# Decimating a complex recurrence by four instead of two: one short scan, three phases by diagonal products on the TensorE, and state reloads on one queue

## The chip, the cores and the metric

The kernel runs on one core of one Trainium2 chip. The metric is the device time of one execution in microseconds (us). Executions of a kernel agree within one or two per cent here (449.45 to 457.46 us for the kernel before), and runs more than 1.5% above the fastest of their kernel are called slow and are left out of ratios. Every ratio below is the mean time of one kernel's fast runs over the mean of the fast runs of the kernel before in the same rounds on the same chip, so it is not quite the ratio of the medians that are quoted. Brackets hold its 95% interval.

Engines: PE is the TensorE's matmuls, PEld its weight loads (they overlap the matmuls: 422.9 and 242.3 us busy in a span of 451.4 us), DVE the VectorE, ACT the ScalarE, POOL the GpSimd, SP the SyncE, which here does nothing but issue DMAs. SPq is its queue. In this code an eviction copies a finished product out of PSUM into SBUF, the on-chip memory; a scatter is a DMA that spreads a result over other partitions; the hole is the one long stretch in which PE stands idle.

## The reference, cut to what matters

S = 2048 steps, D = 1024 channels, P = 1024 complex states, batch 1. Branch a is a complex diagonal recurrence, branch b is a short convolution, a product with v and a long convolution by FFT over 4096 points; a gate mixes both.

```python
def _A_ref(x, ...):
    Lam_bar = jnp.exp(dt * Lam)                       # complex, one per state
    B_bar = ((Lam_bar - 1.0) / Lam)[:, None] * Bmat
    Bu = jnp.einsum("bld,pd->blp", x + 0j, B_bar)
    for t in range(L):
        h = Lam_bar[None, :] * h + Bu[:, t, :]
        hs.append(h)
    return 2.0 * jnp.einsum("blp,dp->bld", hseq, Cmat).real + x * Dskip
def _B_ref(q, k, v, ...):
    kv = k_shift * v                                  # k_shift: 4-tap causal convolution of k
    y = irfft(rfft(kv, 4096) * rfft(ssm_k, 4096))[:S] + kv * ssm_D
    return q * y
g = sigmoid((x * gate_w).sum(-1, keepdims=True))
return g * a + (1 - g) * b                            # q is x
```

## The kernel before

Nearly all big work is matmuls. A small list scheduler in Python (`_Plan`) is given every operation with an engine, a duration, a priority and the buffers it touches; it fixes the order of instructions on every engine, and where each buffer lies in SBUF, before the kernel is built. Some fifty constants (priorities, numbers of buffers) steer it. An elementwise operation with `alt=("POOL", ...)` may be given to POOL instead of DVE, until the planned time `PUNTIL`.

The states are handled in eight blocks of 128. For each block the 2048 steps are split by parity. Odd steps' inputs are folded into even steps by a product with 128x128 diagonal matrices (a complex factor takes four), a scan on DVE runs over even steps only, after a rotation that makes its factor real, and the odd steps follow by another product.

```python
xT = [pl.tile("xT", [2, SE], cap=8) for d in range(ND)]       # SE = 1024, CW = 512, NC = 2
for par in (1, 0):
    for d in range(ND):
        dma("SP", 1.3, ... xT[d].ap[:, par, :] <- xf[par:S:2, d * 128:(d + 1) * 128],
            ..., transpose=True, issue=1.9)                    # 16 transposes of 1024 steps
...
def prep(pi, bn, pr):
    dg = pl.tile("dg", [6, 128], cap=3)                        # six diagonal matrices
    ...
        op("DVE", 0.97, mk(V), ..., alt=("POOL", 1.5, mk(G), PUNTIL))
...
def gemm_u(BT, dg, Hc, par, c, pr, step=8):                    # 16 products B u for 512 steps ...
    ...
    if par == 0:                                               # ... and the odd inputs folded in
        for ri in range(2):
            for k in range(2):
                PE_.matmul(ps.ap[:, ri, 1:CW], lhsT=dg.ap[:, LMAT[ri][k], :],
                           rhs=Hc[c].ap[:, 1, k, 0:CW - 1], ...)
                if c > 0: ...                                  # one column across the seam
...
def rot(Hc, pi, c, tab, wl, pr):                               # DVE, for each chunk c of 512
    ...                                                        # rotate
    V.tensor_tensor_scan(out=W.ap[:, ri, :], data0=col(r2, pi).to_broadcast([128, CW]), ...)
    ...                                                        # rotate back
def odd(dg, Hc, pi, c, pr):
    for ri in range(2):
        PE_.matmul(ps.ap[:, ri, :], lhsT=ident, rhs=Hc[c].ap[:, 1, ri, :], start=True, stop=False)
        for k in range(2):
            PE_.matmul(ps.ap[:, ri, :], lhsT=dg.ap[:, LMAT[ri][k], :], rhs=Hc[c].ap[:, 0, k, :], ...)
    ...
    if pi < NP - NKEEP:                                        # NKEEP = 4 blocks of H stay on chip
        dma(QB, ...)                                           # the others go to HBM
...
for i, pi in enumerate(korder):
    load_CT(pi, 0, CTP(i, 0))                                  # C transposed, first half
    ...
        t = pl.tile("Hr", [2, 2, CW], cap=16, hold=True)
        dma(QB, 1.6, ..., alt=QA)                              # reload, 512 KB; QB, QA = "POOL", "SP"
```

At the end 32 output products of 16 matmuls each (line L1097, L1085 in the changed kernel) contract all eight blocks of H with C. Each needs H of every block and all of C's half. The last units of branch b run beside them; a unit makes several trips: products, an eviction, elementwise work, a DMA that scatters the result over partitions, and a final product (L782, L784 in the changed kernel) that waits for this scatter.

Of the kernel before, what the change touches and what calls it, by code (L numbers as in the profile page):

```python
# [15 lines left out]
MAGIC = 12582912.0  # L16
# [296 lines left out]
def kernel(  # L313
# [31 lines left out]
    SE = S // 2  # L345
    CW = 512
    NC = SE // CW
# [11 lines left out]
    h_scr = dram.tile([NP, NC, 128, 4 * CW], BF16, name="h_scr")  # L359
    g_scr = dram.tile([2, SE], F32, name="g_scr")  # L360
# [42 lines left out]
    dco = parm.tile([128, NP, 6], F32, name="dco")  # L403
# [23 lines left out]
    r2 = small("r2")  # L427
    mul(r2, rv, rv)
# [13 lines left out]
    TS(out=phn, in0=thn, scalar1=-2.0, scalar2=None, op0=ALU.mult)  # L442
# [23 lines left out]
    phU = small("phU")  # L466
    TS(out=phU, in0=phn, scalar1=float(CW), scalar2=None, op0=ALU.mult)
    rqU = small("rqU")
    TS(out=rqU, in0=phU, scalar1=MAGIC, scalar2=-MAGIC, op0=ALU.add, op1=ALU.add)
    TT(out=phU, in0=phU, in1=rqU, op=ALU.subtract)  # L470
    sU = small("sU")
    nc.scalar.activation(out=sU, in_=phU, func=ACT.Sin, scale=TWO_PI)
    faU = small("faU")
    nc.scalar.activation(out=faU, in_=phU, func=ACT.Abs)
    cU = small("cU")
    nc.scalar.activation(out=cU, in_=faU, func=ACT.Sin, bias=pihalf_col, scale=-TWO_PI)
    msU = small("msU")
    TS(out=msU, in0=sU, scalar1=-1.0, scalar2=None, op0=ALU.mult)
# [47 lines left out]
    XE = -856.08  # L526
    F1P = -578.83
    NSPL = 1
    NWARM = 12
    GP0 = -22.93  # L530
    GP1 = -182.81
    GP2 = -79.99
    BNCAP = 31
    PUNTIL = 41.5
    ZBCAP = 2
    NKEEP = 4
    HCAP = 5
    TABCAP = 15
    ZCAP = 20
    KVCAP = 23  # L540
    QQCAP = 6
    RACAP = 15
    RBCAP = 13
    KTCAP = 1
    ABCAP = 1
    PPCAP = 1
# [3 lines left out]
    S0 = 29.93  # L550
    S1 = 1.34
    C0 = 39.78
    C1 = 2.56
    CB1 = -1.01
    CT0 = 218.24
    CT1 = 3.6
    CT2 = 310.87
    SPARE = 1
    NBIG = 3
    HR0 = 41.49  # L560
    HRc = -154.4
    KP0 = -267.98
    KP1 = -0.01
    KPu = -27.09
    KA0 = -122.57
    VA0 = -112.74
    FN0 = -2.02
    TB0 = -166.71
    TB1 = 13.16
    XS0 = -149.35  # L570
    PN0 = -1.23
    RT0 = 13.76
    OD0 = -6.8
    UE0 = 6.92
    D10 = -557.08
    SC1 = 2.49
# [11 lines left out]
    xT = [pl.tile("xT", [2, SE], cap=8) for d in range(ND)]  # L588
    for par in (1, 0):
        for d in range(ND):  # L590
            dma("SP", 1.3, lambda d=d, par=par: [xT[d].ap[:, par, :]],
                lambda d=d, par=par: [xf[par:S:2, d * 128:(d + 1) * 128]], [], [(xT[d], par)], (-1000 if par else XE) + d, transpose=True, issue=1.9)
# [222 lines left out]
    def s5(prio):  # L815
        LMAT = ((3, 5), (4, 3))
# [7 lines left out]
        def prep(pi, bn, pr):  # L824
            dg = pl.tile("dg", [6, 128], cap=3)
            def mk(eng):
                return lambda: eng.tensor_tensor(out=dg.ap, in0=ident.unsqueeze(1).to_broadcast([128, 6, 128]),
                                                 in1=dco[:, pi, :].unsqueeze(2).to_broadcast([128, 6, 128]), op=ALU.mult)
            if pi == 0:
                for k in range(2):  # L830
                    def part(k=k):
                        V.tensor_tensor(out=dg.ap[:, 3 * k:3 * k + 3, :], in0=ident.unsqueeze(1).to_broadcast([128, 3, 128]),
                                        in1=dco[:, pi, 3 * k:3 * k + 3].unsqueeze(2).to_broadcast([128, 3, 128]), op=ALU.mult)
                    op("DVE", 0.5, part, r=[e_dco], w=[(dg, k)], prio=pr - 5)
            else:
                op("DVE", 0.97, mk(V), r=[e_dco], w=[(dg, 0), (dg, 1)], prio=pr - 5, alt=("POOL", 1.5, mk(G), PUNTIL))
# [39 lines left out]
        def gemm_u(BT, dg, Hc, par, c, pr, step=8):  # L876
            ps = pl.psum([2, CW])
            c0 = c * CW

            def part(ds):  # L880
                def f():
                    for ri in range(2):
                        for d in ds:
                            PE_.matmul(ps.ap[:, ri, :], lhsT=BT.ap[:, d, ri, :], rhs=xT[d].ap[:, par, c0:c0 + CW],  # L884
                                       start=(d == 0), stop=(par == 1 and d == ND - 1))
                op("PE", 2 * len(ds) * MM(512), f, r=[BT] + [(xT[d], par) for d in ds], w=[ps], prio=pr)
            for d0 in range(0, ND, step):
                part(range(d0, d0 + step))
            if par == 0:
                def g():  # L890
                    for ri in range(2):
                        for k in range(2):
                            lm = dg.ap[:, LMAT[ri][k], :]
                            PE_.matmul(ps.ap[:, ri, 1:CW], lhsT=lm, rhs=Hc[c].ap[:, 1, k, 0:CW - 1], start=False,  # L894
                                       stop=(c == 0 and k == 1))
                            if c > 0:
                                PE_.matmul(ps.ap[:, ri, 0:1], lhsT=lm, rhs=Hc[c - 1].ap[:, 1, k, CW - 1:CW],
                                           start=False, stop=(k == 1))
                op("PE", 4 * MM(511) + (0.2 if c else 0), g, r=[(dg, 1), (Hc[c], 1)] + ([(Hc[c - 1], 1)] if c else []), w=[ps],
                   prio=pr)  # L900
            evac(lambda: Hc[c].ap[:, par], lambda: ps.ap, r=[ps], w=[(Hc[c], par)], prio=pr)

        def rot(Hc, pi, c, tab, wl, pr):
            t1 = pl.tile("ra", [2, CW], cap=RACAP)
            t2 = pl.tile("rb", [2, CW], cap=RBCAP)
            H = Hc[c]
# [15 lines left out]
            def g():  # L922
                init = (0.0, 0.0)
                if c > 0:
                    STT = V.scalar_tensor_tensor
                    wb, wi, tq = wl.ap[:, 0:2], wl.ap[:, 2:4], wl.ap[:, 4:6]
                    TS(out=tq, in0=wb, scalar1=col(cU, pi), scalar2=None, op0=ALU.mult)
                    STT(out=wi[:, 0:1], in0=wb[:, 1:2], scalar=col(msU, pi), in1=tq[:, 0:1], op0=ALU.mult, op1=ALU.add)
                    STT(out=wi[:, 1:2], in0=wb[:, 0:1], scalar=col(sU, pi), in1=tq[:, 1:2], op0=ALU.mult, op1=ALU.add)
                    init = (wi[:, 0:1], wi[:, 1:2])  # L930
                for ri in range(2):
                    V.tensor_tensor_scan(out=W.ap[:, ri, :], data0=col(r2, pi).to_broadcast([128, CW]),
                                         data1=t1.ap[:, ri, :], initial=init[ri], op0=ALU.mult, op1=ALU.add)
                if c < NC - 1:
                    V.tensor_copy(wl.ap[:, 0:2], W.ap[:, :, CW - 1])
# [28 lines left out]
        def gates(pr):  # L964
            for par in (1, 0):
                gate1(par, pr[par])
# [17 lines left out]
        def gate1(par, pr):  # L984
# [13 lines left out]
            if par == 1:  # L998
                wps = pl.psum([128])
# [158 lines left out]
```

## Time and profile before

| | kernel before |
|---|---|
| time, median of 3 | 453.71 us (451.0 to 455.12) |
| span of the profiled run | 451.4 us |
| PE, DVE, ACT, POOL busy | 94%, 77%, 65%, 7% |
| mean granted clock | 0.986 |

These are lines of the page of the kernel before: busy time and share of each engine, and PE, POOL and the granted clock in 40 slices of 11.3 us (tenths).

```profile
PE 422.9 (94%) x2859; PEld 242.3 (54%) x2906; DVE 345.6 (77%) x624; ACT 291.2 (65%) x330; POOL 32.6 (7%) x49
...
PE   8799999999999999998999999199999999999995
...
POOL 9800101000101000000000002000000000000000
PEclk9999999999999999999999999779999999999999
```

PE is the engine that bounds, with one hole (the 1) near 280 us. This is a line of PE's timeline in the kernel before: start, us, engine, line, operation, out<-in, shapes, how many.

```profile
321.71 3.62 PE L1097 MATMUL ps<-slab,slab 128*128 128x512 bf16 x16
```

The page gives 379 ns as the mean of one such matmul, but matmuls overlap. Sixteen of them took 3.62 us, of which the last one's own 0.38 us belong to its end, so they start every (3.62 - 0.38) / 15 = 0.216 us: this is the price of 512 streamed columns. With this price one can count what PE really streams in each stage, and what is missing. These are stretches of the kernel before: window, its length, then busy us (count) of PE, PEld, DVE, ACT and POOL, granted clock, DMA share, GB/s.

```profile
20.00:60.00 40.00, 37.23 (x203) 16.64 (x207) 30.00 (x49) 31.75 (x32) 3.60 (x6) 1.00 0.95 182
60.00:120.00 60.00, 57.88 (x411) 34.90 (x418) 56.45 (x98) 50.03 (x53) 5.41 (x10) 1.00 0.82 187
120.00:280.00 160.00, 155.80 (x1134) 94.76 (x1150) 145.04 (x266) 136.74 (x149) 6.38 (x12) 1.00 0.73 159
280.00:300.00 20.00, 9.93 (x68) 5.84 (x67) 7.37 (x13) 7.86 (x10) 0.00 (x0) 0.74 0.96 269
300.00:360.00 60.00, 58.98 (x445) 36.75 (x450) 53.07 (x88) 39.09 (x45) 0.00 (x0) 1.00 0.75 166
```

At 280 to 300 us PE is busy 9.93 of 20 us, and the clock falls to 0.74. The waits of PE in the kernel before name the cause (us in total, times, longest):

```profile
PE ps L782 <- DMA slab<-slab: 11.1, 2, 10.0
PE ps L990 <- DMA slab<-in_A_x_dram: 3.1, 2, 2.2
```

Final products of a unit waited 10.0 us for their scatter. These are lines of the timeline of SP in the kernel before (start, us, what was issued), and after them one of POOL's:

```profile
276.89 5.88 SPq L509 DMA_DIRECT2D slab<-slab  x4
...
286.03 6.71 SPq L509 DMA_DIRECT2D slab<-h_scr  x2
```

```profile
276.63 2.62 POOL L509 DMA_DIRECT2D slab<-h_scr  x5 [0.33 <-PE ps L884]
```

The four parts of the scatter were issued at 276.89, just when POOL issued five reloads of 512 KB in a row.

### The profile page before, as it was taken

The page shows a single profiled execution, that of the slowest core. Times are in us where ns is not written, and L with a number is a line of the kernel's source. Part 1 is how long each engine was busy: PE and PEld are TensorE (multiplying, and loading weights), DVE is VectorE, ACT ScalarE, POOL GpSimd, SP SyncE. Part 2 cuts the span into 40 slices and gives each one's busy share as a digit, 9 for nine tenths or more (in the row PEclk, how much of TensorE's full clock was granted, in tenths as well). Part 3 has the DMA queues.
Part 4 walks back from the last instruction along what each step waited for, and adds up shares of the span by engine and source line. Part 5 has one row for each costly group of instructions (what it writes and reads, how often), then busy time and mean ns, then how long its engine had stood idle before and what let it go on. Part 6 is the DMA issues. An engine that isn't in the chain of part 4 may idle for free.

```text
span 451.4 us, 7616 instructions
## 1 busy us (share of the span) xinstructions
PE 422.9 (94%) x2859; PEld 242.3 (54%) x2906; DVE 345.6 (77%) x624; ACT 291.2 (65%) x330; POOL 32.6 (7%) x49
## 2 busy tenths in 40 slices
PE   8799999999999999998999999199999999999995
PEld 6533546665656546655665566155576544444442
DVE  5974999989999599988998889079998654464412
ACT  3675979887888978997888878268576122321200
POOL 9800101000101000000000002000000000000000
PEclk9999999999999999999999999779999999999999
DMA  8999574899867967494457389988866676353111
GB/s 155 99 249 223 96 198 129 187 239 166 214 157 162 261 134 188 102 229 101 111 158 130 84 153 257 291 212 160 168 149 163 174 206 168 118 163 94 55 39 46
DMA packets 169401, 72.12 MB, mean 160 GB/s; under 512 B 136514, under 2 KB 165202, under 8 KB 169364
## 3 DMA queue, kind: packets, MB, share of 16 engines
q1 hardware_dynamic: 165796, 59.80, 63.3%
q0 software_dynamic: 3504, 11.82, 8.1%
q8 instruction: 23, 0.38, 0.4%
q14 instruction: 14, 0.11, 0.1%
q10 hardware_dynamic: 64, 0.01, 0.0%
HBM read 29.65 MB, written 16.79 MB: 103 GB/s over the span
## 4 chain that ended last, share of the span: by engine, by line
PE 72%; DMA 10%; ACT 7%; SPq 6%; DVE 3%; issue 2%; DVEq 0%; ACTq 0%
PE ps L1097 24%; PE ps L884 20%; DMA slab<-slab 5%; ACT slab L514 5%; SPq L507 5%; PE ps L736 4%; PE ps L737 3%; PE ps L956 3%; PE ps L723 3%; PE ps L763 2%; PE ps L738 2%; DMA kv_scr<-slab 2%; PE ps L894 2%; DMA slab<-in_A_x_dram 2%; PE ps L782 2%
## 5 line engine op out<-in xcount | busy, mean ns | idle before, releaser
L514 ACT CAST slab<-ps 128x1024 bf16<-128x1024 f32 x217 | 205.5, 1032 | 82.4 <-PE ps L765 20.9
L884 PE MATMUL ps<-slab,slab 128*128 128x512 bf16 x486 | 114.1, 379 | 2.8 <-ACT slab L514 1.7
L1097 PE MATMUL ps<-slab,slab 128*128 128x512 bf16 x487 | 109.0, 379 | 0.5
L1097 PEld LDWEIGHTS <-slab 128*128 128x128 bf16 x512 | 49.9, 98 | 59.0 <-issue 0.2
L884 PEld LDWEIGHTS <-slab 128*128 128x128 bf16 x512 | 48.8, 98 | 59.4 <-issue 7.3
L1103 DVE SCALAR_TENSOR_TENSOR slab<-ps,gcols,slab 128x512 bf16<-128x512 f32 x32 | 23.2, 747 | 51.2 <-PE ps L1097 51.1
L1080 ACT ACTIVATE slab<-slab,omgc 128x512 bf16<-128x512 bf16 x32 | 21.3, 735 | 43.7 <-DMA slab<-pB_scr 43.7
L736 PE MATMUL ps<-slab,fC 128*128 128x512 bf16 x115 | 43.5, 379 | 0.8 <-DVE slab L1103 0.5
L514 DVE CAST slab<-ps 128x1024 bf16<-128x1024 f32 x23 | 27.9, 1221 | 11.0 <-PE ps L846 2.9
L737 PE MATMUL ps<-slab,fS 128*128 128x256 bf16 x128 | 34.9, 272 | 0.7
L738 PE MATMUL ps<-slab,fN 128*128 128x256 bf16 x128 | 34.9, 272 | 0.0
L723 PE MATMUL ps<-tab,slab 128*128 128x128 bf16 x512 | 34.0, 220 | 0.7 <-ACT slab L514 0.6
L723 PEld LDWEIGHTS <-slab 128*128 128x128 bf16 x512 | 31.0, 99 | 4.5 <-issue 1.3
L708 ACT ACTIVATE slab<-slab,skc 128x1024 bf16<-128x1024 bf16 (+3 forms) x28 | 32.2, 1164 | 0.2 <-DVE slab L710 0.2
L763 PE MATMUL ps<-slab,gC 128*128 128x256 bf16 x128 | 29.9, 273 | 1.9 <-ACT slab L514 1.4
L710 DVE TENSOR_TENSOR slab<-slab,slab 128x1024 bf16<-128x1024 bf16 (+3 forms) x45 | 30.7, 683 | 0.3 <-ACT slab L708 0.2
L765 PE MATMUL ps<-slab,gS 128*128 128x128 bf16 x128 | 28.0, 219 | 0.0
L764 PE MATMUL ps<-slab,gN 128*128 128x128 bf16 x128 | 28.0, 219 | 0.0
L753 DVE TENSOR_TENSOR slab<-slab 128x512 bf16<-128x512 bf16 x64 | 25.1, 417 | 0.3 <-DMA slab<-slab 0.2
L782 PE MATMUL ps<-slab,tabFc 128*128 128x512 bf16 x32 | 13.1, 409 | 11.1 <-DMA slab<-slab 11.1
L750 DVE TENSOR_TENSOR slab<-slab 128x1024 bf16<-128x1024 bf16 x32 | 21.9, 684 | 1.3 <-PE ps L956 1.3
L1085 DVE SCALAR_TENSOR_TENSOR slab<-slab,gcols,slab 128x512 bf16<-128x512 bf16 x32 | 22.4, 744 | 0.0
(178 smaller groups left out, 536.9 us busy)
## 6 DMA issues: line engine op xcount, KB each, us to landing
slab<-in_A_x_dram SPq DMA_DIRECT2D x32, 256.0 KB
slab<-slab SPq DMA_DIRECT2D x128, 64.0 KB
slab<-in_B_ssm_k_dram SPq DMA_DIRECT2D x8, 512.0 KB
kv_scr<-slab SPq DMA_DIRECT2D x8, 512.0 KB
h_scr<-slab POOLq DMA_DIRECT2D x8, 512.0 KB, 4.1
slab<-kv_scr SPq DMA_DIRECT2D x8, 512.0 KB
pB_scr<-slab SPq DMA_DIRECT2D x16, 256.0 KB
slab<-pB_scr SPq DMA_DIRECT2D x16, 256.0 KB
```

The costliest lines, as they stand in the source:

```text
L514: op("ACT", 1.04, lambda: A.copy(o_(), i_()), r=r, w=w, prio=prio, alt=("DVE", 1.2, lambda: V.tensor_copy(o_(), i_())))
L708: alt=("ACT", 1.17, lambda: A.activation(out=tmp.ap[:, 0:n], in_=kT.ap[:, src], func=ACT.Copy, scale=skc[:, u, j:j + 1])))
L710: op("DVE", 0.7, lambda: TT(out=acc.ap[:, lo:hi], in0=acc.ap[:, lo:hi], in1=tmp.ap[:, 0:n], op=ALU.add), r=[acc, tmp], w=[acc], prio=pr)
L723: PE_.matmul(ps.ap[:, i, :], lhsT=a.ap[:, 8 * q + i, :], rhs=t1v[:, hh * 128:(hh + 1) * 128], start=True, stop=True)
L736: PE_.matmul(ps.ap[:, i], lhsT=fC[:, k2, :], rhs=zz, start=True, stop=False)
L737: PE_.matmul(ps.ap[:, i, :, 0, :], lhsT=fS[:, k2, :], rhs=zz[:, :, 1, :], start=False, stop=False)
L738: PE_.matmul(ps.ap[:, i, :, 1, :], lhsT=fN[:, k2, :], rhs=zz[:, :, 0, :], start=False, stop=True)
L763: PE_.matmul(ps.ap[:, i], lhsT=gC[:, k2, :], rhs=pp.ap[:, i], start=True, stop=False)
L764: PE_.matmul(ps.ap[:, i, 0, :], lhsT=gN[:, k2, :], rhs=pp.ap[:, i, 1, :], start=False, stop=False)
L765: PE_.matmul(ps.ap[:, i, 1, :], lhsT=gS[:, k2, :], rhs=pp.ap[:, i, 0, :], start=False, stop=True)
L884: PE_.matmul(ps.ap[:, ri, :], lhsT=BT.ap[:, d, ri, :], rhs=xT[d].ap[:, par, c0:c0 + CW], start=(d == 0), stop=(par == 1 and d == ND - 1))
L1097: PE_.matmul(ps.ap[:, ti, :], lhsT=Hr[pi, a // 4].ap[:, par, ri, (a % 4) * 128:(a % 4 + 1) * 128], rhs=CT[pi, dh].ap[:, ri, :], start=(i = ...
```

## The change

The intent is to halve DVE's part of the recurrence. With four phases instead of two parities, one scan of 512 steps per block does what two scans of 512 did. PE pays: 12 diagonal matmuls instead of 8 fold three phases into phase 0, and a chain of three products of six matmuls each, with an eviction after each, gives the phases 1 to 3 instead of two products. H of six blocks instead of four stays on chip, so that four reloads are left instead of eight, and all four are issued by SP. x comes in as 32 transposes of 512 steps instead of 16 of 1024. `PUNTIL` rises, so POOL may take elementwise work longer. All constants were tuned again.

```diff
-    xT = [pl.tile("xT", [2, SE], cap=8) for d in range(ND)]
-    for par in (1, 0):
+    xT = [pl.tile("xT", [NPH, CW], cap=8) for d in range(ND)]          # NPH = 4
+    for ph in (1, 2, 3, 0):
         for d in range(ND):
-            dma("SP", 1.3, lambda d=d, par=par: [xT[d].ap[:, par, :]], ... xf[par:S:2, ...], issue=1.9)
+            dma("SP", 0.65, lambda d=d, ph=ph: [xT[d].ap[:, ph, :]], ... xf[ph:S:NPH, ...], issue=1.0)
...
-            dg = pl.tile("dg", [6, 128], cap=3)
+            dg = pl.tile("dg", [12, 128], cap=DGCAP)
+            def part(k, n, eng, dur, **kw):
+                ...
+                op("DVE", dur, f(V), ..., alt=("POOL", 1.9 * dur, f(G), PUNTIL))
+            part(0, 3, V, 0.5)
+            part(3, 9, V, 1.4)
...
-                        for k in range(2):                              # fold one phase: 4 matmuls
-                            PE_.matmul(ps.ap[:, ri, 1:CW], lhsT=lm, rhs=Hc[c].ap[:, 1, k, 0:CW - 1], ...)
+                        for j in range(1, NPH):                         # fold three phases: 12 matmuls
+                            for k in range(2):
+                                PE_.matmul(ps.ap[:, ri, 1:CW], lhsT=dg.ap[:, LM(j, ri, k), :],
+                                           rhs=H[(NPH - j) // 2].ap[:, (NPH - j) % 2, k, 0:CW - 1], ...)
...
-            for c in range(NC):
-                rot(Hc, pi, c, tab, wl, prio(b + RT0 + 4 * c))
-            for c in range(NC):
-                odd(dg, Hc, pi, c, prio(b + OD0 + 2 * c))
+            rot(Hc, pi, tab, prio(b + RT0))
+            for ph in (1, 2, 3):
+                chain(dg, Hc, ph, prio(b + OD0 + 2 * (ph - 1)))
...
-                    dma(QB, 1.6, ... h_scr[pi, c], ..., alt=QA)         # reload
+                    dma("SP", 1.8, ... h_scr[pi, c], ...)
...
-                        for _ in range(20):                             # warm-up matmuls
+                        for _ in range(12):
...
-    PUNTIL = 41.5
-    NKEEP = 4
-    CT0 = 218.24
+    PUNTIL = 126.82
+    NKEEP = 6
+    CT0 = 313.99                                                        # priority of C's transposes
...                                                                      # and about 45 more constants
```

## The prediction

> **What bounds it now.** PE. The busy table gives it 94%, but matmul ends are modelled, so I counted streamed columns: at 0.213 us for 512 columns (page's groups: 109 us for 512 output products) the program's order holds 406 us of columns, 9.8 of them warm-up, in a span of 451.4. The windows view shows the rest: 0-44 us (x and B arrive; last x at 43.8), PE busy 97% from 44 to 280, one hole at 280-300 (PE busy 9.9 of 20 us, granted clock 0.74), then PE full to 447. The waits view has one large PE wait after the start: 10.0 us of the final inverse matmuls for slab<-slab, the scatter of the inverse. By the timeline eight 512 KB reloads of H start around it, six in a burst on the POOL queue. DVE (77%) and ACT (65%) cost PE only waits under 1 us.
>
> **What the change does.**
> - PE: per 128 states 12 diagonal matmuls for phase 0 instead of 8, and 18 in the chain instead of 12: +80 x 0.213 = +17 us, all on the bounding engine. 32 one-column matmuls go, ~0.1 us each: -3. Eleven more switches to the one-row gate product, ~0.2 each: +2.
> - DVE: half of the rotations and scans go: per 512 steps 4 x 0.684 + 4 x 0.42 + 2.45 = 6.9 us, x 8 = -55 us, and -5 of seam work; but 29 more evictions stand on DVE (x 1.22 = +35). [...] DVE does not bound: worth 1-3 us.
> - DMA: H of six of eight state blocks stays on chip; four reloads instead of eight, in order on SP. The 10 us wait and the low clock after it (13 us of columns missing in 280-300) should mostly go: -9 to -13. But scatters now stand behind reloads and C transposes; between a unit's last inverse product and its final product only 8-11 us of columns lie (18.6 at the old hole): new waits of 1-5 us.
> - Start: 32 half-size x transposes. C transposes of that size take 1.2 us to issue, the large ones 1.28, so the last x lands at 44-47 us though the first phase is complete at about 15 instead of 27. Both orders place equal PE work before the last piece: -2 to +2.
>
> **Sum.** 451 + 17 - 3 + 2 - 12 - 2 + 1 = about 454; perfect packing would give 444. I put the time at **452 us**, 8 in 10 between **444 and 462**. Chances: faster by over 2% 0.10, within 2% 0.78, slower by over 2% 0.12.
>
> **What would show it.** PE columns up by 14 us, PE share 95% or more; DVE busy down by only 20-40 us; no PE wait of 10 us around the first output products, and full clock there, but waits of 1-5 us of final products for slab<-slab; last gate product at 44-47 us; the output stage starts later with fewer other matmuls inside.
>
> **What would make it wrong.** Faster: PE streams from 17 us and loses nothing later. Slower: the serial chain (scan, three products, an eviction between each) leaves PE nothing else ready; reloads waiting on SP for buffers block the scatters and open a new hole of 10 us; or half-size transposes cost more than half.

The prediction's small prices against the trace of the kernel before: a scan took 1.21 to 1.27 us (L932). The issue of a transpose of C took 1.20 to 1.21 us and that of a large one of x 1.30 us (medians). The two steps of a switch, from a product of 512 columns to the one-row gate product and back, took 0.309 and 0.310 us from start to start instead of 0.216, 0.19 us more in sum. The 0.1 us of a one-column matmul was the estimate: its weight load took 0.096 us (L897), but the next matmul starts 0.026 us after it.

## The result, and the profile after

The changed kernel is correct and slower.

| | before | after |
|---|---|---|
| time, median of 6 | 452.95 us | 466.82 us |
| ratio of fast runs | | 1.0336 [1.0274, 1.0398] |
| span of the profiled run | 451.4 us | 465.5 us |
| mean granted clock | 0.986 | 0.983 |

The same lines of the page, after:

```profile
PE 437.9 (94%) x2839; PEld 246.6 (53%) x2890; DVE 340.3 (73%) x552; ACT 269.6 (58%) x300; POOL 55.7 (12%) x54
...
PE   7869999889999999999999999996998999999995
...
POOL 9940103080251000000000000000000000000000
PEclk9897999998999999999999999999999999999999
```

PE's share is the same, and the hole near 280 us is gone. New dents stand near the start and near 315 us, and POOL is busy up to 140 us (the 8 and the 5). The stretches of the changed kernel (columns as before):

```profile
20.00:60.00 40.00, 35.63 (x174) 14.40 (x177) 32.85 (x46) 28.58 (x33) 10.31 (x10) 0.91 0.78 166
60.00:120.00 60.00, 56.01 (x394) 34.35 (x400) 56.17 (x79) 42.18 (x45) 15.33 (x13) 0.97 0.66 156
120.00:280.00 160.00, 158.95 (x1098) 94.42 (x1118) 140.61 (x225) 126.74 (x137) 11.60 (x9) 1.00 0.67 146
280.00:300.00 20.00, 19.84 (x153) 12.37 (x154) 8.87 (x15) 12.60 (x13) 0.00 (x0) 1.00 0.96 189
300.00:360.00 60.00, 52.13 (x409) 33.13 (x416) 42.67 (x65) 35.45 (x38) 0.00 (x0) 1.00 0.77 164
```

And the waits of PE in the changed kernel:

```profile
PE ps L980 <- ACT slab L514: 4.1, 1, 4.1
PE ps L725 <- DMA slab<-kv_scr: 3.6, 1, 3.6
PE ps L765 <- DVE slab L755: 3.3, 2, 2.4
PE ps L784 <- DMA slab<-slab: 2.8, 2, 1.8
PE ps L980 <- DMA slab<-in_A_x_dram: 2.6, 3, 1.1
```

Instead of one wait of 10 us there are five or six of 1 to 4 us. To add them up I counted, for each stage, the columns that PE streamed (records of weight loads by line, times the columns of that line, at 0.2133 us for 512, without the fixed part of a matmul) and took them from the length of the stage. Both parts of the price are read from the kernel before: its matmuls of 512 columns start 215.8 ns apart (mean of neighbours of L1097 from 120 to 440 us) and those of 128 columns 55.8 ns apart (L723; the group of 16 at 268.97 us took 1.06 us, (1.06 - 0.22) / 15 = 0.056). So 384 columns took 160.0 ns, which is 0.2133 us for 512, and about 2.5 ns are left that do not go with the columns. Warm-up matmuls do not count as useful. The rest is time that PE lacks, whether it waited, ran at a low clock (0.50 from 34 to 40 us, below) or paid the fixed part of each matmul. The 2.5 us that the changed kernel lacks from 120 to 280 us, with 1118 weight loads, are about this fixed part (an estimate: 1118 x 2.5 ns = 2.8 us): there the trace shows no wait of PE.

| lost in the stage, us | 0-20 | 20-60 | 60-120 | 120-280 | 280-300 | 300-360 | 360-end | sum | useful columns |
|---|---|---|---|---|---|---|---|---|---|
| before | 16.4 | 5.2 | 4.0 | 8.3 | 13.0 | 2.2 | 6.1 | 55.0 | 396.4 |
| after | 16.2 | 10.8 | 6.5 | 2.5 | 0.5 | 9.1 | 6.5 | 52.0 | 413.5 |
| difference | -0.2 | +5.6 | +2.5 | -5.8 | -12.5 | +6.9 | +0.4 | -3.0 | +17.1 |

The 14.1 us are 17.1 us of added columns less only 3.0 us of lost time won back. The hole gave its 12.5 us, but 5.6 us more are lost at 20-60 and 6.9 us more at 300-360.

Three readings show what stands there. First, x. The timeline of SP shows the issue of all transposes of x as one group, in the kernel before and then in the changed kernel:

```profile
0.73 36.41 SPq L507 DMA_TRANSPOSE slab<-in_A_x_dram  x16
```

```profile
0.73 43.73 SPq L507 DMA_TRANSPOSE slab<-in_A_x_dram  x32
```

The same 4 MB take 43.73 instead of 36.41 us: on average 1.37 us for a transpose of half the size, against 2.28 (43.73 / 32 and 36.41 / 16; the medians of a single issue are 1.26 and 1.30 us, the longest 2.2 and 6.8). The last gate product, which needs the last piece, ran at 49.3 instead of 43.8 us.

Second, DVE and POOL. The table computation of the FFT has the same tiny instruction in both kernels (16 elements per partition). Here it is in the kernel before, then two lines of DVE in the changed kernel, then what POOL did meanwhile in the changed kernel:

```profile
13.72 0.23 DVE L618 TENSOR_SCALAR slab<-iota_row,slab 128x16 f32<-128x16 f32 x1
```

```profile
21.12 3.96 DVE L620 TENSOR_SCALAR slab<-iota_row,slab 128x16 f32<-128x16 f32 x1
...
101.52 3.76 DVE L708 TENSOR_SCALAR slab<-slab,skc 128x1024 bf16<-128x1024 bf16 x1
```

```profile
14.85 6.15 POOL L832 TENSOR_TENSOR slab<-ident,dco 128x1152 bf16<-128x1152 bf16 x3 [0.82 <-DVE dco L477]
...
22.13 2.91 POOL L832 TENSOR_TENSOR slab<-ident,dco 128x384 bf16<-128x384 bf16 x2
...
102.07 2.91 POOL L832 TENSOR_TENSOR slab<-ident,dco 128x384 bf16<-128x384 bf16 x2
```

A DVE instruction of 0.23 us lasted 3.96 us until POOL's group at 22.13 had ended at 25.04, and the one of 3.76 us (0.48 us in after_no_pool below) ended at 105.28, after POOL's group at 102.07 had ended at 104.98. So these two ended only when POOL's products had ended; below this is called the stall. Not every instruction stalls: three products of DVE at 94.78, 96.53 and 97.14 us, beside POOL's work from 94.64 to 99.61 us, took their usual 0.68 to 0.69 us. What decides this is not shown. By their records the two start before POOL's products (21.12 against 22.13 us, 101.52 against 102.07), while POOL is still issuing DMAs. That the issuing is not the cause is shown by after_no_pool below, where POOL issues such loads beside DVE instructions (14.90 to 16.00 us, 99.33 to 100.40) and these keep their usual lengths (0.15 to 1.36 us). ACT's tables come from these DVE results. They stood in ACT's order ahead of the eviction of the gate's row, so this came at 34.12 us and PE waited 4.07 us for it, as these lines of PE in the changed kernel show (the wait stands in brackets):

```profile
28.75 2.33 PE L884 MATMUL ps<-slab,slab 128*128 128x512 bf16 x10
35.15 2.29 PE L980 MATMUL ps<-slab,gwb 128*1 128x512 bf16 x5 [4.07 <-ACT slab L514]
```

After it the granted clock read 0.50 from 34 to 40 us, and eight products of 256 columns took 1.89 us there (37.38 us) instead of 1.05 (24.08 us, clock 1.00). In the old hole, with its wait of 10.0 us, the clock read 0.50 from 292 to 296 us. In the changed kernel it read 0.50 from 106 to 108 us after a wait of 2.44 us, which ended at 105.7 us, but after one of 3.6 us, which ended at 325.6 us, it stayed at 1.00. The length of a wait alone does not decide here.

Third, the output products. These are their first groups on PE's timeline, before and after:

```profile
307.45 7.07 PE L1097 MATMUL ps<-slab,slab 128*128 128x512 bf16 x31
```

```profile
334.82 6.85 PE L1085 MATMUL ps<-slab,slab 128*128 128x512 bf16 x31
```

They begin 27 us later, while the whole kernel is only 14 us longer. Counted in the order of the program, other matmuls worth 126 products of 512 columns stood behind the first output product before; now it is 58. (The texts below count 114 and 54, and 77, 51 and 66 for other kernels, because they take the inverse products of 4 x (256 + 128 + 128) columns as three instead of four. By columns these are 84, 56 and 74.)

### The profile page after: what moved, and what is told of

The parts are those of the page before. It is cut to its first block, busy times and chain, and to the rows that moved or that the text cites. A ratio compares the mean times of both kernels' runs of the same rounds, so it can differ in the third digit from the quotient of the medians.

```text
span 465.5 us, 7526 instructions
## 1 busy us (share of the span) xinstructions
PE 437.9 (94%) x2839; PEld 246.6 (53%) x2890; DVE 340.3 (73%) x552; ACT 269.6 (58%) x300; POOL 55.7 (12%) x54
## 4 chain that ended last, share of the span: by engine, by line
PE 81%; DVE 9%; DMA 3%; ACT 3%; issue 2%; SPq 1%; POOL 0%; DVEq 0%; POOLq 0%
PE ps L1085 23%; PE ps L884 20%; PE ps L738 5%; PE ps L725 5%; PE ps L894 4%; PE ps L949 4%; PE ps L765 3%; PE ps L739 3%; PE ps L740 3%; PE ps L847 3%; PE ps L947 2%; PE ps L767 1%; PE ps L766 1%; DMA slab<-slab 1%; PE ps L784 1%
## 5 line engine op out<-in xcount | busy, mean ns | idle before, releaser
L514 ACT CAST slab<-ps 128x1024 bf16<-128x1024 f32 x196 | 190.7, 1018 | 112.7 <-PE ps L785 16.7
L884 PE MATMUL ps<-slab,slab 128*128 128x512 bf16 x487 | 126.9, 380 | 1.3 <-issue 0.2
L1085 PE MATMUL ps<-slab,slab 128*128 128x512 bf16 x501 | 110.9, 379 | 0.8 <-DVE slab L1091 0.2
L514 DVE CAST slab<-ps 128x1024 bf16<-128x1024 f32 x52 | 63.3, 1222 | 29.1 <-PE ps L884 6.7
L1091 DVE SCALAR_TENSOR_TENSOR slab<-ps,gcols,slab 128x512 bf16<-128x512 f32 x32 | 23.2, 747 | 58.1 <-PE ps L1085 56.0
L738 PE MATMUL ps<-slab,fC 128*128 128x512 bf16 x120 | 46.0, 383 | 1.3 <-DVE slab L514 1.2
L725 PE MATMUL ps<-tab,slab 128*128 128x128 bf16 x512 | 37.2, 219 | 3.6 <-DMA slab<-kv_scr 3.6
L712 DVE TENSOR_TENSOR slab<-slab,slab 128x1024 bf16<-128x1024 bf16 (+3 forms) x48 | 35.7, 750 | 0.1
L751 DVE TENSOR_TENSOR slab<-slab 128x1024 bf16<-128x1024 bf16 x32 | 21.9, 685 | 6.6 <-DMA slab<-slab 5.1
L710 ACT ACTIVATE slab<-slab,skc 128x1024 bf16<-128x1024 bf16 (+3 forms) x22 | 25.0, 1155 | 1.4 <-DVE slab L712 1.2
L949 PE MATMUL ps<-slab,slab 128*128 128x512 bf16 x82 | 24.9, 379 | 0.3
L1073 DVE SCALAR_TENSOR_TENSOR slab<-slab,gcols,slab 128x512 bf16<-128x512 bf16 x28 | 19.6, 745 | 4.2 <-ACT slab L1068 4.2
```

The costliest lines, as they stand in the source:

```text
L514: op("ACT", 1.04, lambda: A.copy(o_(), i_()), r=r, w=w, prio=prio, alt=("DVE", 1.2, lambda: V.tensor_copy(o_(), i_())))
L712: op("DVE", 0.7, lambda: TT(out=acc.ap[:, lo:hi], in0=acc.ap[:, lo:hi], in1=tmp.ap[:, 0:n], op=ALU.add), r=[acc, tmp], w=[acc], prio=pr)
L725: PE_.matmul(ps.ap[:, i, :], lhsT=a.ap[:, 8 * q + i, :], rhs=t1v[:, hh * 128:(hh + 1) * 128], start=True, stop=True)
L738: PE_.matmul(ps.ap[:, i], lhsT=fC[:, k2, :], rhs=zz, start=True, stop=False)
L884: PE_.matmul(ps.ap[:, ri, :], lhsT=BT.ap[:, d, ri, :], rhs=xT[d].ap[:, ph, :], start=(d == 0), stop=(ph > 0 and d == ND - 1))
L949: PE_.matmul(ps.ap[:, ri, :], lhsT=dg.ap[:, LM(1, ri, k), :], rhs=Hp.ap[:, (ph - 1) % 2, k, :], start=False, stop=(k == 1))
```

## The experiments

All experiments keep one of the two kernels and edit it in one point. Where the scheduler would have planned everything anew, its plan was frozen and only the emission was edited, except in the last three, where the plan is the point.

| run | correct | median us | ratio to before |
|---|---|---|---|
| after | yes | 466.82 | 1.0336 [1.0274, 1.0398] |
| after_less80 | no | 460.17 | 1.0168 [1.0107, 1.0229] |
| before_more80 | yes | 464.80 | 1.0274 [1.0224, 1.0323] |
| before_tiny_reload | no | 442.61 | 0.9774 [0.9695, 0.9853] |
| before_late_reload | yes | 455.83 | 1.0045 [0.9966, 1.0123] |
| after_no_pool | yes | 464.75 | 1.0237 [1.0219, 1.0255] |
| after_kv_early | yes | 469.14 | 1.0320 [1.0258, 1.0383] |
| after_warm20 | yes | 465.91 | 1.0274 [1.0212, 1.0336] |
| before_reload_ordered | yes | 450.95 | 0.9907 [0.9837, 0.9976] |
| after_big_x | yes | 474.76 | 1.0471 [1.0407, 1.0534] |
| after_no_pool_big_x | yes | 477.77 | 1.0512 [1.0428, 1.0595] |
| after_tiny_reload | no | 465.87 | 1.0260 [1.0193, 1.0327] |
| before_half_x | yes | 457.84 | 1.0099 [1.0039, 1.0160] |
| after_tiny_C | no | 466.38 | 1.0284 [1.0224, 1.0343] |
| after_no_pool_less80 | no | 452.70 | 0.9998 [0.9943, 1.0052] |
| before_reload_ordered2 | yes | 453.09 | 0.9949 [0.9882, 1.0017] |
| before_keep6 | yes | 470.12 | 1.0444 [1.0359, 1.0530] |
| before_late_C | yes | 468.67 | 1.0396 [1.0305, 1.0488] |
| after_earlier_C | yes | 465.46 | 1.0321 [1.0258, 1.0384] |

The median of the kernel before was 452.5 to 454.5 us in all rounds. Two kernels of different rounds are compared by their ratios.

### What do the 80 added products cost?

**after_less80** leaves out 80 of the changed kernel's diagonal products (the result is wrong by 3.5%):

```diff
-                        for j in range(1, NPH):
+                        for j in range(1, NPH - 1):
...
-                    for k in range(2):                        # in chain
+                    for k in range(1):
```

> The changed kernel with the 80 added recurrence matmuls left out and nothing else moved (wrong result on purpose): 4 of the 12 diagonal products of phase 0 and 6 of the 18 of the chain per 128 states are not issued, the order of all other instructions is that of the changed kernel. Theory 1 (PE streams almost all the time, so its columns are the time): 80 x 0.213 = 17 us less, a span of about 448 against 465.5, ratio to the kernel before about 0.995. Rival (the time is set by the serial chain of scan, evictions and transfers, and the products hide in its waits): under 5 us less, ratio above 1.02.

The ratio fell from 1.0336 to 1.0168, which is 7 to 8 us and less than half of 17. The span of its profile fell only from 465.5 to 460.4.

**before_more80** adds 80 products to the kernel before, whose results are overwritten:

```diff
                 for ri in range(2):                           # in odd
+                    for _ in range(3 - ri):
+                        PE_.matmul(ps.ap[:, ri, :], lhsT=ident, rhs=Hc[c].ap[:, 1, ri, :], start=True, stop=True)
                     PE_.matmul(ps.ap[:, ri, :], lhsT=ident, rhs=Hc[c].ap[:, 1, ri, :], start=True, stop=False)
```

> The kernel before with 80 more 512-column matmuls in the odd-step product (each bank is written once or more before its real start, so the result stays right) and nothing else moved. Theory 1: +17 us, minus what hides in the 10 us hole (nothing, as all 80 lie before it): ratio 1.035 to 1.04, a span of about 468. Rival (PE has slack): ratio below 1.01.

It is 2.7% slower (464.80 us; the span went from 451.4 to 463.0, which is 11.6 us for 17 us of columns). The price of the products is therefore real but not full. From 20 us on, its lost time fell from 38.8 to 33.0 us by the same count as above (3.9, 3.7, 6.0, 5.3, 7.7 and 6.4 in its six stages): some of the added columns ran where PE had lacked work.

**after_no_pool_less80** does the same to the changed kernel after POOL's work beside DVE is taken away (see after_no_pool below), and leaves the 80 out:

> The changed kernel without GpSimd elementwise work after the first phase table (that alone: 1.0237) and without the 80 added products (that alone 1.0168; wrong result on purpose). [...]more than 6.6 us less than without GpSimd work alone, 10 to 14 us, ratio 0.993 to 1.003. If the price of the products stays at 6.6 us: ratio 1.009.

Here leaving them out brought the ratio from 1.0237 to 0.9998, which is about 11 us. So the products cost 11 to 12 us in two of three places, and 7 to 8 in the plain changed kernel, where, without them, waits took their room: from 300 to 360 us it lacked 13.3 instead of 9.1 us.

### What was the hole worth, and what made it?

**before_tiny_reload** cuts each reload to 16 KB (wrong result):

```diff
-  dma(QB, 1.6, lambda t=t: [t.ap.rearrange("p a b s -> p (a b s)")], lambda pi=pi, c=c: [h_scr[pi, c]], ...
+  dma(QB, 1.6, lambda t=t: [t.ap.rearrange("p a b s -> p (a b s)")[:, 0:64]], lambda pi=pi, c=c: [h_scr[pi, c][:, 0:64]], ...
```

> The kernel before with each H reload cut from 512 KB to 16 KB, same queues and order (wrong result on purpose). If the 10 us PE wait for the scatter is caused by the bytes of the reload burst, that wait shrinks below 2 us, the clock stays full at 280-300 us and the time falls by 10 to 13 us (ratio 0.971 to 0.978). If the scatter was late for another reason (its own issue, SP queue), the wait stays and the ratio is above 0.99.

The time fell by 2.3%. This is the wait's line in its profile:

```profile
PE ps L782 <- DMA slab<-slab: 2.6, 1, 2.6
```

The wait fell from 10.0 to 2.6 us with the same number of DMAs on the same queues: the bytes of the reloads held the scatter up. Over 280 to 360 us it lacks 6.6 us of columns (4.6 and 2.0) where the kernel before lacks 15.2. So the hole was worth about 10 us, as the prediction had it.

**before_late_reload** takes half of the bytes away from there: four of the eight reloads are moved to SP, each behind one of the first output products.

> The kernel before with the four reloads of the second half of the sequence moved from the burst to the SP queue, one after each of the first four output products; their slots and all else unchanged, result right. If the burst causes the hole, half of it (2 MB less before the scatter) should leave a wait of 2 to 5 us instead of 10 and the kernel becomes 5 to 11 us faster (ratio 0.975 to 0.99). If the bytes don't matter, ratio 1.0.

This did not help (1.0045, and the interval holds 1). The wait was still 8.8 us. Half of the burst is enough to hold the scatter up, so the wait does not scale with the bytes.

**before_reload_ordered** keeps all bytes and changes only the order: all eight reloads go to SP, four of them right behind the four parts of the awaited scatter, and four after the first output products.

```diff
+    for j in range(4):
+        o = pl.reloads[j, 1]; o.fn = o.fnalt; order.remove(o)
+        order.insert(order.index(pl.ones[j]) + 1, o)
+    for j in range(4):
+        o = pl.reloads[j, 0]; o.fn = o.fnalt; order.remove(o)
+        order.insert(order.index(pl.scat[4, 3]) + 1 + j, o)
```

> The kernel before with all eight H reloads on the SP queue, in order: four right behind the scatter that PE waited for at 283-293 us, four one by one after the first output products; nothing else moved, result right. If the reload burst ahead of and beside that scatter makes the hole (16 KB reloads took it from 10 to 2.6 us; moving half of the bytes away left 8.8), the wait falls to 2 to 4 us, and the kernel is 5 to 11 us faster than the kernel before (ratio 0.976 to 0.99), the fastest of all. If the scatter is held by the transposes and conv loads ahead of it on its own queue, the wait stays near 9 us and the ratio is 1.0.

It is correct and 0.9% faster than the kernel before (5 rounds, interval 0.2 to 1.6%), which is 4 us where 5 to 11 were expected, and the lowest ratio of a correct kernel here. The order on SP in its profile, and then its waits:

```profile
276.81 3.06 SPq L510 DMA_DIRECT2D slab<-slab  x4
279.97 2.59 SPq L510 DMA_DIRECT2D slab<-h_scr  x4
```

```profile
PE ps L764 <- DVE slab L754: 4.4, 1, 4.4
PE ps L783 <- DMA slab<-slab: 3.1, 1, 3.1
```

The wait for the scatter is 3.1 instead of 10.0 us, but a wait of 4.4 us at 338 us is new. Over 280 to 360 us it lacks 14.7 us (5.3 and 9.4) against 15.2: most of the hole moved back by 50 us. **before_reload_ordered2** spreads the four late reloads otherwise (behind output products 1, 1, 2 and 3):

> As before_reload_ordered (0.991), but the four late reloads stand after output products 1, 1, 2 and 3 instead of 1, 2, 3 and 4. The 4.4 us wait that was new there (338 us) came from a reload ahead of a store of pB whose buffer DVE needed; it should go, and the kernel should be 3 to 5 us faster than that one: ratio 0.98 to 0.985. If another wait takes its place: 0.99.

It was not better (0.9949, its interval holds 1), with waits of 4.6 us for scatters and 3.3 us for DVE. The place where the late reloads do no harm was not found.

**after_tiny_reload** does the cut to 16 KB in the changed kernel (wrong result), to see if the four reloads that are left make its new waits at 300 to 360 us:

> The changed kernel with its four H reloads cut from 512 KB to 16 KB, same queue and order (wrong result on purpose). If the waits at 300-360 us (3.6 us for the kv load, 2.8 us for scatters) come from the reloads' bytes that are still ahead of them on the one SP queue: 4 to 7 us faster than the changed kernel (ratio 1.018 to 1.025). If they come from the C transposes packed there and from the order of issue: under 2 us (1.029 or more).

They hardly do: the wait for kv was 2.6 and the longest wait for a scatter 2.3 us, from 300 to 360 us it lacks 8.5 instead of 9.1 us, and the ratio (1.0260) has an interval that overlaps that of the changed kernel.

### The start: transposes, DVE beside POOL, the warm-up

**before_half_x** splits each transpose of x in the kernel before into two:

```diff
-  lambda d=d, par=par: [xf[par:S:2, d * 128:(d + 1) * 128]], ...
+  lambda d=d, par=par: [xf[h * SE + par:(h + 1) * SE:2, d * 128:(d + 1) * 128] for h in range(2)], ...
```

> The kernel before with each of its 16 x transposes of 1024 steps split in two of 512, nothing else changed, result right: this part of the change alone. If half-size transposes cost 1.37 us each against 2.28 for a whole one: x is there 5 to 7 us later (last gate product near 50 us instead of 44) and the kernel is 3 to 7 us slower (ratio 1.007 to 1.016). If the x load is bound by bytes alone: no change.

It is 1.0% slower (interval 0.4 to 1.6%), about 4.5 us. Issue of x takes 46.46 us, as the timeline of SP in it shows:

```profile
0.73 46.46 SPq L507 DMA_TRANSPOSE slab<-in_A_x_dram  x32
```

The last gate product came at 48.6 instead of 43.8 us, and from 20 to 60 us it lacks 9.0 instead of 5.2 us. Small transposes alone therefore make most of the loss that the changed kernel shows in this stage (10.8).

**after_big_x** goes the other way: the changed kernel with 16 transposes of 1024 steps, of which PE reads every second column for its phase.

```diff
-  rhs=xT[d].ap[:, ph, :]
+  rhs=xph(d, ph)        # v[:, ph // 2:2 * CW:2] of the pair of phases loaded together
```

> The changed kernel with x loaded as in the kernel before, 16 transposes of 1024 steps instead of 32 of 512; PE reads every second column of them; order of all else as in the changed kernel, result right. If the half-size transposes cost more than half (1.37 us each against 2.28): x is all there about 5 us earlier (last gate product at 44 instead of 49) and the kernel is 1 to 4 us faster than the changed one (ratio 1.025 to 1.031). If DVE's late tables are what holds the start, or if reading every second column slows the products: no gain or a loss.

It is worse than the changed kernel, 1.0471. The issue of x is short again (34.7 us), but its order of products asks first for phase 1 alone, and the last piece of this now reaches PE at 21.9 instead of 15.3 us; the last gate product ran at 52.5 us, where 44 was expected. The mean record of the products B u is also longer (388 instead of 380 ns). Which of the two costs the time was not separated. An order of products made for phases cannot take back the large transposes for free. **after_no_pool_big_x** joins it with the next edit:

> Both together: no GpSimd elementwise work after the first phase table, and large x transposes. In the run without GpSimd work PE waited 7.9 us in 11 pieces for x, so the two parts should add up: 7 to 10 us faster than the changed kernel (ratio 1.012 to 1.019). If the x wait is only bandwidth, the result is that of the first alone, 1.024.

It gave 1.0512, again worse; its profile fell in a slow run, so only the time is used.

**after_no_pool** gives POOL's elementwise work after the first phase table back to DVE, in the same places of the order:

```diff
+    for o in order:
+        if o.eng == "POOL" and o.dma is None and o.fnalt is o.fn and o.start > 12.0:
+            o.fn = o.fn0
```

> The changed kernel with the elementwise work that GpSimd (POOL) does after its first phase table (diagonal builds and three more phase tables, about 25 us of POOL) given to DVE at the same places of the order; all else unchanged, result right. Theory A ([...]16 to 1024 elements took 3 to 4 us there instead of 0.2 to 0.5): DVE's table preparation ends near 18 us instead of 25.5, PE's 4.1 us wait at 31-35 us and 2.4 us wait at 102 us and the low clock after them go; 5 to 10 us faster than the changed kernel, ratio to the kernel before 1.012 to 1.024. Rival (DVE is simply given more work at the start, so taking POOL's share too makes it later): not faster, ratio 1.033 or above.

The clause that is cut told the stall of DVE beside POOL as a rule; the trace shows it for single instructions (3.96 and 3.76 us above), and "there" means beside POOL's work.

It is correct, at 1.0237 instead of 1.0336, at the lower end of what was expected: about 1% or 4.5 us. The two instructions that had lasted 3.96 and 3.76 us are short in its profile, though DVE has more to do:

```profile
16.62 0.24 DVE L621 TENSOR_SCALAR slab<-iota_row,slab 128x16 f32<-128x16 f32 x1
...
100.57 0.48 DVE L709 TENSOR_SCALAR slab<-slab,skc 128x1024 bf16<-128x1024 bf16 x1
```

The wait of 4.1 us for the gate's row and the one of 2.4 us at 103 us are gone. From 60 to 120 us it lacks 2.0 instead of 6.5 us, all of the loss that was new there. From 20 to 60 us it still lacks 10.1 us: in place of one wait it has eight for x, 4.9 us in all (eleven and 7.9 us with those before 20 us). There the late x is what bounds, and the stall of DVE only stood in front of it. By the intervals of the two ratios the gain is 1.5 to 7.5 us; the span of the profile fell by 2.8 us.

**after_warm20** restores 20 warm-up matmuls instead of 12 per piece:

> The changed kernel with 20 instead of 12 warm-up matmuls after each gate product of the first phase, as the kernel before has; nothing else. If the low clock at 12-18 us costs time: clock full there and up to 1 to 2 us faster than the changed kernel (ratio 1.029 to 1.032). If the start is bound by the arrival of x and by DVE: no change, 1.033.

It gave 1.0274, 0.6% less, with an interval that overlaps that of the changed kernel: a gain is not shown. (The low clock of the expectation: the changed kernel reads 0.77, 0.50 and 0.88 in the three stretches of 2 us from 12 to 18 us, the kernel before 1.00. With 20 matmuls the page gives 9 tenths for the slice from 11.6 to 23.2 us, where the changed kernel's gives 8.) The 3.9 us wait for the row is still there.

### The waits between 300 and 360 us

**after_kv_early** moves the load that PE waits 3.6 us for to the earliest place that its single buffer allows, which is one place ahead:

> The changed kernel with the last load of kv moved ahead of the loads before it on the SP queue to the point where its buffer is free; all else unchanged. If the 3.6 us PE wait at 322 us comes from the place of this load behind the C transposes on the one queue: that wait goes, 2 to 4 us faster than the changed kernel (ratio 1.025 to 1.03). If the load waits for its data or buffer: no change (1.033). If moving it only by one place is possible, little changes either.

The wait was 2.6 us, others grew (11.5 us lacking in the stage), and the time was the same (1.0320). **after_tiny_C** cuts the first 16 transposes of C, which fill SP's queue here, to 64 rows (wrong result):

> The changed kernel with its first 16 C transposes cut from 512 to 64 rows, same queue and order (wrong result on purpose). In the changed kernel they stand between 300 and 335 us on the SP queue, in the kernel before from 221 us on. If they hold the kv load and the scatters there: PE's waits of 3.6 and 2.8 us at 300-350 us shrink below 2 us in sum, the columns missing at 300-360 us fall from 9 to about 4, and the kernel is 3 to 6 us faster than the changed one (ratio 1.020 to 1.027). If DVE's or the evictions' order is behind it: no change.

The same again (1.0284; waits of 3.6 and 1.8 us, 8.8 us lacking). With after_tiny_reload this makes three single suspects that change little. But in all three the order of PE was frozen. What they could not test is whether PE merely had nothing to put into these round trips, because the output products began late. The last three runs plan anew.

**before_keep6** is the kernel before with one constant of the change:

```diff
-    NKEEP = 4
+    NKEEP = 6
```

> The kernel before with one constant of the change alone: H of six blocks is kept on chip instead of four (the scheduler plans again; four reloads are left, most still on the POOL queue). In the plan the first C transposes and the first output product move later: 77 instead of 114 products' worth of other matmuls are left behind the first output product (54 in the changed kernel). Theory: the new waits over 300 to 360 us of the changed kernel come from this: the kept blocks fill SBUF, C comes in late, the output products start late and are missing as work beside the last transforms' round trips. Then the 10 us hole mostly goes, but 2 to 6 us of new PE waits appear after 290 us (kv load, scatters, evictions): 444 to 450 us. Rival: the new waits belong to the chain of phases, not to the kept blocks: the hole goes and nothing comes, 440 to 444 us.

It is correct and 4.4% slower than the kernel before. The old hole shrank (9.7 us lacking from 280 to 300 instead of 13.0, and a wait for a scatter of only 0.6 us in its list), but look at the stretch:

```profile
300.00:360.00 60.00, 47.85 (x345) 28.38 (x343) 42.06 (x71) 29.06 (x33) 0.00 (x0) 0.97 0.85 159
```

PE is busy 47.85 of 60 us here. By columns it lacks 16.1 us from 300 to 360, and 25.8 us from 280 to 360 in place of 15.2. The priority of C's transposes is untouched, yet the first of them was issued at 277.5 instead of 220.9 us, and the first output product ran at 318.3 instead of 307.4 us. So keeping two more blocks delays C, with nothing else changed by hand. The expected 444 to 450 us were missed widely: both theories thought that the hole's 10 us would stay won.

**before_late_C** leaves four blocks kept and sets the priority of C's first half as in the changed kernel:

```diff
-    CT0 = 218.24
+    CT0 = 313.99
```

> The kernel before with one constant alone: the priority of the first eight C transposes pairs is that of the changed kernel (313.99 instead of 218.24), so that they are planned late; 51 products' worth of other matmuls are left behind the first output product, as in the changed kernel (54; 114 before). Theory (late output products leave the last transforms without work beside them): PE waits of 4 to 9 us over 300 to 360 us in transforms' lines (kv load, scatters, evictions), 452 to 462 us. Rival (the late output stage is harmless; the waits come from the chain or the phases): waits after 300 us stay under 2 us, 448 to 453 us.

It is 4.0% slower, more than either theory expected. Its waits of PE (the first that are listed), and its stretch:

```profile
PE ps L782 <- DMA slab<-slab: 10.8, 2, 7.2
PE ps L782 <- issue: 2.8, 1, 2.8
PE ps L736 <- ACT slab L514: 2.6, 3, 2.0
```

```profile
300.00:360.00 60.00, 46.96 (x298) 26.67 (x296) 35.15 (x56) 26.97 (x31) 0.00 (x0) 0.86 0.71 151
```

Output products began at 325.4 us, and 20.5 us of columns are missing from 300 to 360 us (28.7 from 280). This kernel has no phases and no chain. A late output stage alone is enough to open waits of this kind, and the rival, a cause in the chain, is not needed for them.

**after_earlier_C** sets the priority in the changed kernel to 280 instead of 313.99; its plan leaves 74 instead of 58 products' worth of other matmuls behind the first output product.

> The changed kernel with one constant alone: priority of the first eight C transposes pairs 280 instead of 313.99; the plan then leaves 66 instead of 54 products' worth of other matmuls behind the first output product. Theory: some of the 9 us of columns missing over 300 to 360 us come back, 1 to 4 us: 463 to 466 us. Rival: no change, 465 to 469 us.

Output products began at 330.7 instead of 334.8 us. From 300 to 360 us it lacks 7.5 instead of 9.1 us, and the kv wait is gone from its list. The ratio is 1.0321, so the gain of time is not shown. With the old priority (218.24) too, the plan of the changed kernel leaves only 70. Whether the six kept blocks hold it there was not run on the chip: a changed kernel with four kept blocks is missing. The scheduler can be replayed without the chip, and its plan answers only in part. With six blocks and the old priority C is in at 306 us and the first output product waits for a reload (313 us). With four, the first transpose of C moves from 277 to 257 us, but the first output product, at 315 us, then waits for one of eight reloads on SP. So in the changed kernel the kept blocks do delay C, but keeping fewer is not planned to bring the output products forward.

Both single-constant edits of the kernel before were planned with constants that had been tuned for its own values, so their full 20 and 18 us (by the ratios) are not the price of the same step inside the changed kernel, where the other constants were tuned with it. What they show is the direction and the mechanism in the kernel before.

## Why the prediction was wrong, point by point

The prediction was 452 us, 444 to 462, and most likely within 2%. The kernel takes 466.8 us, 3.4% more. Its terms against the runs, by columns of PE:

| term in the prediction | predicted, us | found, us |
|---|---|---|
| 80 products on the bounding engine | +17 | +17.1 columns; 11 to 12 of time by adding or removing them, 7 to 8 in the plain changed kernel |
| small terms and DVE (-3, +2, -2) | -3 | -3.3, set against them (60 to 280 us: +2.5 and -5.8) |
| start | -2 to +2 | +5.4 (0 to 60 us) |
| the hole | -12 | -12.5 (280 to 300 us) |
| new waits | +1 | +6.9 (300 to 360 us) and +0.4 (end) |
| sum | +3, put at +1 (452 against 451) | +14 |

- **What bounds.** "PE" was right in both kernels. "PE share 95% or more" was not: it stayed at 94%.
- **The products.** +17 us was right in columns (0.213 us each is one per cent low). As a price in time it was too high (11 to 12 us measured, 7 to 8 in the plain changed kernel), which worked in the kernel's favour: by luck it hid a part of the two misses below.
- **The hole.** "Should mostly go: -9 to -13" was right on its own stage, and before_tiny_reload shows the worth of the hole to be about 10 us. But the prediction put this down to fewer and ordered reloads and did not ask what the room for the kept blocks was used for before.
- **New waits: the first failed step.** The text said "new waits of 1-5 us", said that "the output stage starts later with fewer other matmuls inside", and then entered +1 in the sum. Four waits of 0.8 to 3.6 us came between 300 and 360 us (two of the kind that was named, 1.0 and 1.8 us, and the largest for the load of kv), and over 280 to 360 us the change won 5.6 us, not 12. before_keep6 shows that keeping six blocks pushes C and the output products back, and before_late_C that late output products open waits in the last units' round trips. There the two are one trade, and only its gain was priced. That the 6.9 us of the changed kernel come from it is argued, not shown: after_earlier_C won back 1.6 us of them, and the changed kernel with four kept blocks was not run.
- **Start: the second failed step.** "The last x lands at 44-47 us" was read off C's transposes (1.2 us for the same size). The transposes of x took 1.37 us, and the last gate product ran at 49.3 us. "Half-size transposes cost more than half" had been named as a risk and came true: before_half_x shows about 4.5 us for it alone. The scheduler was told the same too low price: the diff plans 1.0 us of issue for a small transpose and 1.9 for a large one, and 1.37 and 2.28 were measured.
- **POOL was not in the prediction.** The diff raised `PUNTIL` from 41.5 to 126.82 and doubled the diagonal matrices; POOL's busy time rose from 32.6 to 55.7 us. POOL's work with the stalls of DVE beside it cost about 4.5 us (after_no_pool). The plan gives POOL's work a duration and knows no such stall, so it shows free help where there was none. Replayed without the chip, the scheduler plans 448.5 us for the kernel before and 443.3 for the changed one: by its own prices the change is a gain.
- **DVE.** "Down by only 20-40 us" was wrong: it fell by 5.3 us. The added evictions were right (28 to 63 us, 23 to 52 of them). after_no_pool shows DVE at 333.9 us although it does POOL's work too, so stalled instructions (3.96 us for one of 0.23 us) were counted as busy in the changed kernel. The price of a scan was right (2.45 us for two in the prediction; the page has 1.21 to 1.27 us for 512 elements, where a plain product of 512 fp32 elements took 0.69 us), but DVE did not bound, and no run here isolates what its relief bought.

Still open: the -5.8 us from 120 to 280 us were not taken apart by a run. The traces show that in this stretch the kernel before has waits of PE of 3.2 us in sum (five of 0.2 to 0.3 us for evictions by ACT among them) and 20 of the one-column matmuls, and the changed kernel has neither. How much of the 300 to 360 us loss a different tuning could win back, with six kept blocks or with four, is open too, as are the other constants of the diff, which were changed all at once.

## What to carry to other kernels

A buffer that stays on chip takes its room from something else (in before_keep6 two more kept blocks moved the first load of C from 220.9 to 277.5 us): before counting a saved reload as won, look up which later load now has no place and what work waits for it, since the filler lost there can cost as much as the hole that was closed (25.8 us lacking from 280 to 360 us there, 15.2 before). When a change lets GpSimd take elementwise work beside a busy VectorE, look for short VectorE instructions that suddenly last as long as the GpSimd's (0.23 us became 3.96 us here, beside 2.91 us of products), and price them at that. A wait of a small transfer behind a burst of large ones was shortened here by the order of issue (10.0 to 3.1 us) more than by halving the bytes (8.8 us), but check where the moved bytes land.
